# Norms of the later chunks for all heads at once: a fused attention and two-MLP kernel on one core

## The chip, the core and the metric

The kernel runs on one core of one Trainium2 chip. The engines named below are PE (TensorE matmul; PEld is its weight load, which overlaps PE), DVE (VectorE), ACT (ScalarE), POOL (GpSimd) and SP (SyncE), which here issues every transfer between the core's memory and the chip's main memory (DMA). The metric is device time in microseconds (us) of one execution, lower is better.

## What is computed

Cut to what matters, with batch 8, 8 heads, sequence 576, head width 64, so 4608 tokens of 512 values:

```python
kv  = einsum('bhsd,bhse->bhde', k, v)             # no softmax: one 64x64 matrix per head and batch
out = einsum('bhsd,bhde->bhse', q, kv)
rms = sqrt(mean(out * out, axis=-1) + 1e-06)      # over the 64 values of one head
x   = (out / rms * g_norm)                        # -> 4608 x 512
h   = x @ w_in;   x = max(0.01 * h, h) @ w_out            # first MLP, 512 -> 2048 -> 512
h   = x @ w_in2;  x = P(h) / (Q(h) + 1e-6) @ w_out2       # second MLP, P cubic, Q quadratic in |h|
```

## The kernel before

Values lie transposed: features on the 128 partitions, 512 tokens of a chunk in the free dimension. There are nine chunks (numbers 0 to 8) and four feature groups `p` of 128 (two heads each). The weights have 16 blocks of 128 hidden features. Every product of the two MLPs is three matmuls of 128x128 by 512 tokens on type float32r (`mm3`, lines 180 to 182: low weights by high x, high by high, high by low). One block's `emit_h` is 12 of them and its `emit_y` another 12.

A written list of steps, `STARTUP`, makes the attention part of chunks 0 and 1 and the first 6 blocks of both. Then come the units of the first MLP: unit 2 (rest of chunk 0), unit 3 (rest of chunk 1, 10 blocks), and one unit of 16 blocks for each of chunks 2 to 8. A block is a **slot**. In a slot the order on PE is: `emit_h` of the slot's block, `emit_y` of the block two slots earlier, and then what is planned at that slot with the word "pe". `prep(c, ...)` plans the attention part of the next chunk in the slots of the running unit: "load" is issued one slot ahead, "early" is recorded right after `emit_h`, "post" after "pe". The schedule is manual: each engine runs its instructions in the order in which they are written. The second MLP follows with its own loop over all nine chunks; the change doesn't touch it.

For the attention of one chunk `prep` needs, on PE in plain float32: the k v products of a batch (`mm_kv`, line 281, result `kvacc`; five token tiles, the last of 64 tokens, 8 logical matmuls for a pair of column halves each), and q times kv (`mm_out`, line 298, result `po`, once for each pair of feature groups, `mo`). In the before kernel the mean of squares is made for each feature group apart: ACT squares `po` and copies it, the square is split in a high and a low float32r part (ACT, DVE), and `mm_ms` (line 517) multiplies both parts by `ones`, a 128x128 block matrix of 1/64, so that the mean stands in all 64 rows of its head. Then `nm` makes the factor on [128, 512] for each group: two ACT steps (lines 303 and 304) and three DVE steps (lines 307, 308, 311), and splits x.

PSUM tiles of the attention part (`kvacc`, `po`, `pm`) share two banks under the tag "att". The core's four `raw` buffers are shared by the loads of q, k v, the second MLP's weights (32 transfers of 512 KB, three pairs a unit, narrowed on ACT and DVE into `cv` and stored back) and the stores of x.

In units 4 to 7 (chunks 2 to 5) the slots were: `mo` at 2 and 6, `ms` at 4 and 8 (two groups each), k v tiles at 10 (two), 12 (two) and 14 (the last). In unit 3: k v of one batch at 0 and 1, `mo` at 2 and 5, `ms` at 4 and 7, k v of the next batch at 8 and 9. Units 8 and 9 (chunks 6 and 7) have no k v left; the last unit prepares nothing.

Of the kernel before, what the change touches and what calls it, by code (L numbers as in the profile page):

```python
# [8 lines left out]
F32 = mybir.dt.float32  # L9
F32R = mybir.dt.float32r  # L10
U32 = mybir.dt.uint32
I64 = mybir.dt.int64
AF = mybir.ActivationFunctionType
ALU = mybir.AluOpType
# [3 lines left out]
P = 128  # L18
N = 512
# [3 lines left out]
c wu,30 kv,0,3,w0_8 kv,0,4,w0_9 w,2,1 kv,0,2,w0_10 kv,0,1,w0_11 q,0,0,w0_12 kv,0,0,w1_6 q,0,1,w1_7 km,0,3  # L23
    wu,3 km,0,4 wu,3 w,0,1 kv,1,3,w1_8 kv,1,2,w1_9 ab,2,1 g na,2,1 km,0,2 wu,3 w,0,0 kv,1,0,w0_6 kv,1,1,w0_7
    km,0,1 wu,3 hi,2,1 w,1,1 kv,1,4,w1_5 lo,2,1 q,1,0,raw q,1,1,raw w,2,0 km,0,0 wu,3 w,5,1 w,1,0 ev,0 po,0,0
    wu,3 po,0,1 wu,3 sq,0,1 sq,0,0 sq,0,3 pm,0,0 wu,6 sq,0,2 ab,0,1 pm,0,1 wu,6 na,0,1 km,1,3 nr,0 km,1,2 nw,0
    hi,0,1 w,3,1 ab,0,0 cg bc,0,0 na,0,0 oc,0,2,w0_9 oc,0,1,w0_8 km,1,0 oc,0,3,w0_9 oc,0,0,w0_8 km,1,1 xw,0,1
    w,3,0 hi,0,0 xw,0,0 xh,0,1 lo,0,0 ab,1,1 xh,0,0 xl,0,1 km,1,4 na,1,1 ev,1 bc,0,1 po,1,0 xw,0,3 hi,1,1 w,4,1
    xw,0,2 xh,0,3 lo,1,1 sq,1,0 xh,0,2 xl,0,3 po,1,1 sq,1,1 xl,0,2 oc,1,1,w0_10 pm,1,0 xl,0,0 ab,2,0 lo,0,1
    sq,1,3 h,0,0 na,2,0 oc,1,2,w0_11 oc,1,3,w0_11 sq,1,2 ab,1,0 w,5,0 hi,2,0 na,1,0 pm,1,1 oc,1,0,w0_10 lk,0,0  # L30
    h,0,1 lo,2,0 ab,3,1 w,4,0 nr,1 gl,0,0 na,3,1 ab,5,1 ab,3,0 y,0,0 lk,0,1 nw,1 w,6,1 hi,3,1 hi,1,0 na,5,1
    ab,5,0 bc,1,1 h,0,3 xw,1,3 hi,5,1 w,8,1 lo,1,0 xh,1,3 lo,3,1 ab,4,0 xl,1,3 ab,4,1 h,0,2 gl,0,1 xw,1,2
    lo,5,1 xh,1,2 na,3,0 y,0,1 lk,0,2 xl,1,2 w,6,0 hi,3,0 gl,0,2 lk,0,3 lo,3,0 bc,1,0 na,4,1 ab,6,1 y,0,2
    xw,1,0 hi,4,1 w,7,1 xw,1,1 ab,6,0 xh,1,0 lo,4,1 xh,1,1 h,0,4 xl,1,0 xl,1,1 gl,0,3 na,6,0 y,0,3 lk,0,4
# [7 lines left out]
def kernel(  # L42
# [36 lines left out]

    x2 = [dp.tile([P, NC, N], F32, tag=f"x2_{c}", name=f"x2_{c}") for c in range(NCH)]  # L80
    yp = [dp.tile([P, NC, N], F32, tag=f"yp_{c}", name=f"yp_{c}") for c in range(2)]
    w2f = [dp.tile([P, 2, NC * P], F32, tag=f"w2_{f}", name=f"w2_{f}") for f in range(NF)]


# [47 lines left out]
    def split(hi, lo, src, pool=False):  # L132

        nc.scalar.activation(out=hi, in_=src, func=AF.Copy)  # L134
        if pool:
            nc.gpsimd.tensor_tensor(out=lo, in0=src, in1=hi.bitcast(F32), op=ALU.subtract)  # L136
        else:
            split_lo(hi, lo, src)
# [59 lines left out]
    def new_x():  # L198
        return ([xp.tile([P, N], F32R, tag=f"xh{cc}", name=f"xh{cc}") for cc in range(NC)],
                [xp.tile([P, N], F32R, tag=f"xl{cc}", name=f"xl{cc}") for cc in range(NC)])  # L200
# [42 lines left out]
    with tc.manual_schedule():  # L243
        Y = {}
        G = {}
        with ExitStack() as actx:
# [37 lines left out]
            def evac_kv(bt, acc):  # L284
                KV[bt] = kvp.tile([P, NC, D], F32, tag="kv", name="kv")
                nc.scalar.copy(out=KV[bt], in_=acc[:, :NC * D].rearrange("p (c e) -> p c e", c=NC))
# [15 lines left out]
            def norm_act(m, r, w):  # L302
                nc.scalar.activation(out=r, in_=m, func=AF.Abs_reciprocal_sqrt, scale=MS_S, bias=lnb[:, 0:1])
                nc.scalar.activation(out=w, in_=r, func=AF.Square, scale=MS_R)

            def norm_dve(m, r, w):
                nc.vector.scalar_tensor_tensor(out=w, in0=m, scalar=EPS, in1=w, op0=ALU.add, op1=ALU.mult)
                nc.vector.scalar_tensor_tensor(out=w, in0=w, scalar=-3.0, in1=r, op0=ALU.add, op1=ALU.mult)

            def scaled(out, o, w):  # L310
                nc.vector.scalar_tensor_tensor(out=out, in0=o, scalar=gsc[:, 0:1], in1=w, op0=ALU.mult, op1=ALU.mult)


            order = []
            for f in range(NF + 3):
# [79 lines left out]
            def scratch(tag, n, name="s"):  # L395
                return tp.tile([P, N], F32, tag=tag, name=name, bufs=n)
# [2 lines left out]
                return (ps_h if at == "h" else ps_a if at == "att" else ps_y).tile([P, N], F32, tag=at, name=name)  # L399

            def leaky(ps):
                t = scratch("t", 4, "t")
                nc.scalar.activation(out=t, in_=ps, func=AF.Prelu, alpha=0.01)  # L403
                return t

# [22 lines left out]
            def p_po(c, g):  # L428
                for p in (2 * g, 2 * g + 1):
                    po[c, p] = bank(f"y{p}", "po")  # L430
                mm_out(c, g, qs.pop((c, g)), (po[c, 2 * g], po[c, 2 * g + 1]))

            def p_sq(c, p):
                ss[c, p] = scratch("sh" if p % 2 else "sl", 2)
                nc.scalar.activation(out=ss[c, p], in_=po[c, p], func=AF.Square)

            def p_oc(c, p, at):
# [3 lines left out]
                        xx[c, p // 2 * 2 + i] = t[:, i, :]  # L441
                nc.scalar.activation(out=xx[c, p], in_=po[c, p], func=AF.Copy, scale=gsc[:, 0:1])

            def p_pm(c, g):

                if c not in pm:
                    pm[c] = bank("att", "pm")
                for p in (2 * g, 2 * g + 1):
                    nc.tensor.matmul(out=pm[c][32 * p:32 * (p + 1)], lhsT=pick, rhs=ss.pop((c, p)), start=True, stop=True)  # L449

            def p_nr(c):
                rr[c], ww[c] = scratch("s", 1, "r"), scratch("o", 2, "w")
                norm_act(pm[c], rr[c], ww[c])

            def p_nw(c):
# [46 lines left out]
                name, *args = step.split(",")  # L502
                STEPS[name](*(int(x) if x.isdigit() else x for x in args))

            def sq_out(ps, o):

                s = tp.tile([P, N], F32, tag="s", name="s")
                nc.scalar.activation(out=s, in_=ps, func=AF.Square)
                nc.scalar.copy(out=o, in_=ps)
                hi = tp.tile([P, N], F32R, tag="sh", name="sh", bufs=2)  # L510
                lo = tp.tile([P, N], F32R, tag="sl", name="sl", bufs=2)
                split(hi, lo, s)
                return lo, hi

            def mm_ms(parts, dst):
                for i, x in enumerate(parts):
                    nc.tensor.matmul(out=dst, lhsT=ones, rhs=x, start=i == 0, stop=i == len(parts) - 1)  # L517

            def norm(o, ps):
                r = tp.tile([P, N], F32, tag="t", name="r", bufs=4)  # L520
                w = tp.tile([P, N], F32, tag="t", name="w", bufs=4)
                norm_act(ps, r, w)
                norm_dve(ps, r, w)
                scaled(w, o, w)
                return w

            def prep(c, out0, outs, bursts):

                slots = {}

                def at(s, when, fn, *args):
                    slots.setdefault(s, {}).setdefault(when, []).append(lambda: fn(*args))

                st = {}

                def ld(bt, i):
                    st["kv", i] = load_kv(bt, i)

                def mm(bt, i):
                    if i == 0:  # L540
                        acc[bt] = ps_a.tile([P, NC * P], F32, tag="att", name="kvacc")
                    mm_kv(i, st.pop(("kv", i)), acc[bt], i == 0, i == nk - 1)

                for s, bt, tiles in bursts:
                    for i in tiles:
                        at(s, "load", ld, bt, i)
                        at(s, "pe", mm, bt, i)
                        if i == nk - 1:
                            at(s, "post", lambda bt=bt: evac_kv(bt, acc.pop(bt)))

                def new():
                    X[c] = new_x()

                def ldq(g):
                    st["q", g] = load_q(c, g)

                def mo(g):
                    for p in (2 * g, 2 * g + 1):
                        st["po", p] = ps_a.tile([P, N], F32, tag="att", name="po")
                    mm_out(c, g, st.pop(("q", g)), (st["po", 2 * g], st["po", 2 * g + 1]))  # L560

                def so(p):
                    o = tp.tile([P, N], F32, tag="o", name="o", bufs=2)
                    st["s", p] = sq_out(st["po", p], o)
                    st["po", p] = o

                def ms(p):
                    st["pm", p] = ps_a.tile([P, N], F32, tag="att", name="pm")
                    mm_ms(st.pop(("s", p)), st["pm", p])

                def nm(p):
                    if p == 0:
                        new()
                    w = norm(st.pop(("po", p)), st.pop(("pm", p)))
                    split(X[c][0][p], X[c][1][p], w)

                lag = 2
                for g in range(NC // 2):
                    s = out0 + g * outs
                    at(s, "load", ldq, g)  # L580
                    at(s, "pe", mo, g)
                    for i in range(2):
                        p = 2 * g + i
                        at(s + 1, "early", so, p)
                        at(s + lag, "pe", ms, p)
                        at(s + lag + 1 + i * (outs - lag - 1), "early", nm, p)
                return slots

            def run_slot(slots, s, when):
# [22 lines left out]

            for ui, (c, f0, f1) in enumerate(units):
                slots = {}
                tiles = (0, 1), (2, 3), (4,)
                if ui < 2:
                    continue
                if ui == 3:
                    slots = prep(2, 2, 3, [*zip((0, 1, 1), (2, 2, 2), tiles), *zip((8, 9, 9), (3, 3, 3), tiles)])
                elif ui > 3 and c + 1 < NCH:  # L620
                    slots = prep(c + 1, 2, 4, [*zip((10, 12, 14), (c + 2,) * 3, tiles)] if c + 2 < B else [])
                last = ui == len(units) - 1
                for f in range(f0, f1):
                    sl = f - f0
# [187 lines left out]
```

## Time and profile before

| what | value |
|---|---|
| three runs | 1673.28, 1676.21, 1677.27 us, median 1676.21 |
| the profiled execution, its own time | 1677.88 us |
| its span, first to last instruction | 1675.8 us |
| PE busy | 1665.6 us, 99% of the span |
| DVE, ACT, POOL busy | 970.2, 853.6, 168.8 us |
| chain that ended last | PE 96%, DVE 2%, DMA 1% |
| granted TensorE clock | 1.0 in the stretches used below, that is 2.4 GHz |

Matmuls are pipelined, so a record of one is longer than the time that it takes from the stream. What a stretch of PE costs is read here from the starts of the matmuls on either side of it.

### The profile page before, as it was taken

The page shows a single profiled execution, that of the slowest core. Times are in us where ns is not written, and L with a number is a line of the kernel's source. Part 1 is how long each engine was busy: PE and PEld are TensorE (multiplying, and loading weights), DVE is VectorE, ACT ScalarE, POOL GpSimd, SP SyncE. Part 2 cuts the span into 40 slices and gives each one's busy share as a digit, 9 for nine tenths or more (in the row PEclk, how much of TensorE's full clock was granted, in tenths as well). Part 3 has the DMA queues.
Part 4 walks back from the last instruction along what each step waited for, and adds up shares of the span by engine and source line. Part 5 has one row for each costly group of instructions (what it writes and reads, how often), then busy time and mean ns, then how long its engine had stood idle before and what let it go on. Part 6 is the DMA issues. An engine that isn't in the chain of part 4 may idle for free.

```text
span 1675.8 us, 19355 instructions
## 1 busy us (share of the span) xinstructions
PE 1665.6 (99%) x7959; PEld 1355.1 (81%) x7959; DVE 970.2 (58%) x1132; ACT 853.6 (51%) x1150; POOL 168.8 (10%) x74
## 2 busy tenths in 40 slices
PE   8999999999999999999999999999999999999999
PEld 6688788878888887878888888888888888888887
DVE  3949335254352615342347767776767777777776
ACT  3636335253443425343347656666665666656565
POOL 0000000000000000000001122222122222212221
PEclk9999999999999999999999999999999999999999
DMA  9325434142322323020331010101010000101000
GB/s 250 127 88 178 144 91 128 57 139 82 112 86 86 114 72 110 26 89 0 122 106 63 1 51 1 50 1 51 1 48 4 26 26 1 50 1 50 1 25 25
DMA packets 38359, 112.39 MB, mean 67 GB/s; under 512 B 4480, under 2 KB 4480, under 8 KB 38272
## 3 DMA queue, kind: packets, MB, share of 16 engines
q1 hardware_dynamic: 38272, 111.17, 20.8%
q8 instruction: 62, 1.02, 0.3%
q14 instruction: 25, 0.20, 0.0%
HBM read 81.79 MB, written 29.36 MB: 66 GB/s over the span
## 4 chain that ended last, share of the span: by engine, by line
PE 96%; DVE 2%; DMA 1%; ACT 0%; SPq 0%; issue 0%
PE ph L180 16%; PE y L180 15%; PE y L182 15%; PE y L181 15%; PE ph L182 15%; PE ph L181 15%; PE kvacc L281 1%; PE po L298 1%; DMA raw<-in_kv_dram 1%; PE pm L517 1%; PE warm L411 0%; DVE w L130 0%; PE bc L462 0%; DVE tmp L165 0%; PE pm L449 0%; DVE tmp L168 0%
## 5 line engine op out<-in xcount | busy, mean ns | idle before, releaser
L180 PE MATMUL ph<-xh,w 128*128 128x512 f32 x1152 | 452.1, 392 | 1.0 <-DVE w L130 1.0
L182 PE MATMUL ph<-xl,w 128*128 128x512 f32 x1152 | 448.5, 389 | 0.0
L181 PE MATMUL ph<-xh,w 128*128 128x512 f32 x1152 | 448.5, 389 | 0.0
L180 PE MATMUL y<-gh,w 128*128 128x512 f32 x1152 | 448.4, 389 | 0.1
L181 PE MATMUL y<-gh,w 128*128 128x512 f32 x1152 | 448.2, 389 | 0.0
L182 PE MATMUL y<-gl,w 128*128 128x512 f32 x1152 | 448.1, 389 | 0.0
L136 POOL TENSOR_TENSOR gl<-p,gh 128x1024 fp32r<-128x1024 f32 x70 | 168.6, 2408 | 1482.6 <-ACT gh L134 1482.6
L130 DVE TENSOR_TENSOR gl<-t,gh 128x512 fp32r<-128x512 f32 x144 | 99.4, 691 | 351.5 <-ACT gh L639 330.9
L180 PEld LDWEIGHTS ph<-xh,w 128*128 128x128 f32 x1152 | 216.1, 188 | 54.9 <-issue 7.4
L180 PEld LDWEIGHTS y<-gh,w 128*128 128x128 f32 x1152 | 216.3, 188 | 46.0 <-ACT gh L483 0.8
L182 PEld LDWEIGHTS y<-gl,w 128*128 128x128 f32 x1152 | 216.3, 188 | 45.1 <-DVE gl L130 0.2
L182 PEld LDWEIGHTS ph<-xl,w 128*128 128x128 f32 x1152 | 216.2, 188 | 45.1
L181 PEld LDWEIGHTS ph<-xh,w 128*128 128x128 f32 x1152 | 216.5, 188 | 44.4
L181 PEld LDWEIGHTS y<-gh,w 128*128 128x128 f32 x1152 | 216.0, 188 | 44.8
L403 ACT ACTIVATE t<-ph 128x512 f32<-128x512 f32 x144 | 85.5, 594 | 314.5 <-PE ph L182 314.5
L690 ACT ACTIVATE e<-ph,bb 128x1024 f32<-128x1024 f32 (+1 forms) x73 | 80.6, 1105 | 291.2 <-PE ph L182 291.2
L693 DVE SCALAR_TENSOR_TENSOR e<-s,b,e 128x1024 f32<-128x1024 f32 (+1 forms) x73 | 92.6, 1269 | 176.6 <-ACT s L691 176.6
L701 DVE SCALAR_TENSOR_TENSOR e<-e,z 128x1024 f32<-128x1024 f32 (+1 forms) x73 | 104.8, 1436 | 30.6 <-ACT z L698 30.5
L700 DVE SCALAR_TENSOR_TENSOR p<-p,na,ph 128x1024 f32<-128x1024 f32 (+1 forms) x73 | 92.4, 1266 | 2.6
L702 DVE SCALAR_TENSOR_TENSOR p<-p,na,z 128x1024 f32<-128x1024 f32 (+1 forms) x73 | 91.9, 1259 | 0.0
L703 DVE SCALAR_TENSOR_TENSOR p<-e,p 128x1024 f32<-128x1024 f32 (+1 forms) x73 | 88.3, 1210 | 2.5
L699 DVE TENSOR_TENSOR p<-p,ph 128x1024 f32<-128x1024 f32 (+1 forms) x73 | 87.5, 1198 | 0.0
(83 smaller groups left out, 1248.7 us busy)
## 6 DMA issues: line engine op xcount, KB each, us to landing
raw<-in_kv_dram SPq DMA_DIRECT2D x32, 512.0 KB, 4.5
tmp<-in_w_dram SPq DMA_DIRECT2D x32, 512.0 KB, 5.6
raw<-in_w_dram SPq DMA_DIRECT2D x32, 512.0 KB, 6.1
raw<-in_qT_dram SPq DMA_DIRECT2D x36, 256.0 KB, 5.8
x<-raw SPq DMA_DIRECT2D x18, 512.0 KB, 3.4
raw<-x SPq DMA_DIRECT2D x18, 512.0 KB, 5.4
w<-cv SPq DMA_DIRECT2D x16, 512.0 KB, 2.9
raw<-w SPq DMA_DIRECT2D x32, 256.0 KB, 3.2
```

What stands on the lines that cost most here:

```text
L130: nc.vector.tensor_tensor(out=lo, in0=src, in1=hi.bitcast(F32), op=ALU.subtract)
L136: nc.gpsimd.tensor_tensor(out=lo, in0=src, in1=hi.bitcast(F32), op=ALU.subtract)
L180: nc.tensor.matmul(out=dst, lhsT=wl, rhs=xh, start=first, stop=False, **kw)
L181: nc.tensor.matmul(out=dst, lhsT=wh, rhs=xh, start=False, stop=False, **kw)
L182: nc.tensor.matmul(out=dst, lhsT=wh, rhs=xl, start=False, stop=last, **kw)
L403: nc.scalar.activation(out=t, in_=ps, func=AF.Prelu, alpha=0.01)
L693: nc.vector.scalar_tensor_tensor(out=e, in0=s, scalar=b1[:, 0:1], in1=e, op0=ALU.mult, op1=ALU.add)
L699: nc.vector.tensor_tensor(out=p, in0=p, in1=ph, op=ALU.mult)
L700: nc.vector.scalar_tensor_tensor(out=p, in0=p, scalar=na[:, 1:2], in1=ph, op0=ALU.add, op1=ALU.mult)
L701: nc.vector.scalar_tensor_tensor(out=e, in0=e, scalar=Q_C, in1=z, op0=ALU.add, op1=ALU.mult)
L702: nc.vector.scalar_tensor_tensor(out=p, in0=p, scalar=na[:, 0:1], in1=z, op0=ALU.add, op1=ALU.mult)
L703: nc.vector.scalar_tensor_tensor(out=p, in0=e, scalar=-2.0, in1=p, op0=ALU.add, op1=ALU.mult)
```

## The change

For chunks 2 to 8 the mean square is now made as chunks 0 and 1 already made it: ACT's squares of all four groups lie in one tile `sq`, and four plain float32 matmuls with `pick` (128x32; columns 0 and 1 hold 1/64 for one head each) put the means of all eight heads in one PSUM bank, group `p` in rows 32p and 32p+1. One `nm` makes the factor for all heads on one [128, 512] tile. A store writes it to main memory (`rs`), and two loads read it back so that each head's row stands in 64 partitions for all four groups. `sx` then multiplies and splits x for each group. The gain `g_norm` is applied by the ACT copy out of `po`. The slots move too: in units 4 to 7 `mo` at 2 and 5, `ms` with three k v tiles right behind it at 8, the spread at the end of slot 9, the other two k v tiles at 11, and the four `sx` at 12 to 15; in unit 3 `mo` at 2 and 3, `ms` with three tiles at 4, the spread at 5, two tiles at 7, `sx` at 8 and 9. Two scratch tiles of `STARTUP` get other homes, and the scratch `t` has 3 buffers in place of 4.

```diff
-            def mm_ms(parts, dst):
-                for i, x in enumerate(parts):
-                    nc.tensor.matmul(out=dst, lhsT=ones, rhs=x, start=i == 0, stop=i == len(parts) - 1)
+            def mm_ms(p, x, dst):
+                nc.tensor.matmul(out=dst[32 * p:32 * (p + 1)], lhsT=pick, rhs=x, start=True, stop=True)
...
-                t = scratch("t", 4, "t")
+                t = scratch("t", 3, "t")
...
+                def so(p):
+                    if p == 0:
+                        st["s"] = squares()
+                        st["o"] = tp.tile([P, NC, N], F32, tag="o", name="o")
+                    ps = st.pop(("po", p))
+                    nc.scalar.activation(out=st["s"][:, p, :], in_=ps, func=AF.Square)
+                    nc.scalar.activation(out=st["o"][:, p, :], in_=ps, func=AF.Copy, scale=gsc[:, 0:1])
+                def ms():
+                    st["m"] = ps_a.tile([P, N], F32, tag="att", name="pm")
+                    for p in range(NC):
+                        mm_ms(p, st["s"][:, p, :], st["m"])
+                def nm():
+                    r, w = scratch("t", 3, "r"), scratch("t", 3, "w")
+                    norm_act(st["m"], r, w)
+                    norm_dve(st.pop("m"), r, w)
+                    st["w"] = w
+                def spread_w():
+                    nc.sync.dma_start(out=rs[c], in_=st.pop("w"))
+                    t = st["b"] = squares()
+                    for j in range(P // D):
+                        nc.sync.dma_start(out=t[j * D:(j + 1) * D], in_=rs[c].rearrange("(p r) n -> r p n", r=32)[j:j + 1]
+                                          .to_broadcast([D, NC, N]))
+                def sx(p):
+                    if p == 0:
+                        X[c] = new_x()
+                    x = st["o"][:, p, :]
+                    nc.vector.tensor_tensor(out=x, in0=x, in1=st["b"][:, p, :], op=ALU.mult)
+                    split(X[c][0][p], X[c][1][p], x)
...
-                    slots = prep(2, 2, 3, [*zip((0, 1, 1), (2, 2, 2), tiles), *zip((8, 9, 9), (3, 3, 3), tiles)])
+                    slots = prep(2, (2, 3), 4, (8, 8, 9, 9), [(0, 2, (0, 1)), (1, 2, (2, 3, 4)), (4, 3, (0, 1, 2)), (7, 3, (3, 4))])
...
-                    slots = prep(c + 1, 2, 4, [*zip((10, 12, 14), (c + 2,) * 3, tiles)] if c + 2 < B else [])
+                    slots = prep(c + 1, (2, 5), 8, (12, 13, 14, 15), [(8, c + 2, (0, 1, 2)), (11, c + 2, (3, 4))] if c + 2 < B else [])
```

PE in the unit of chunk 2. Before, the means of two feature groups stand alone between the last `y` of a slot and the first `ph` of the next (slot 4), and the k v products of two tiles stand alone at slot 10.

```order
L182 MATMUL y_2088<-gl,w_2_579 128x512
L517 MATMUL pm<-sl,ones 128x512
L517 MATMUL pm<-sh,ones 128x512
L517 MATMUL pm<-sl,ones 128x512
L517 MATMUL pm<-sh,ones 128x512
L180 MATMUL ph<-xh_1728,w_5_762 128x512
```

In the changed kernel, slot 8 of the same unit:

```order
L183 MATMUL y_2046<-gl,w_6_1019 128x512
L448 MATMUL pm<-sq,pick 32x512 x4
L282 MATMUL kvacc<-raw 64x64 x24
L181 MATMUL ph<-xh_1884,w_9_1065 128x512
L182 MATMUL ph<-xh_1884,w_9_1065 128x512
```

The eight float32r matmuls of a chunk in two places became four plain float32 ones of 32 output rows in one place, with three k v tiles (24 logical matmuls) behind them.

SP, the only queue that issues transfers, in the same unit, from the second pair of weight loads on; `w_N<-cv` is the store of a narrowed weight block. Before:

```order
L209 DMA w_0_86<-cv 128x1024
L147 DMA raw<-in_w_dram 128x512 x4
L263 DMA raw<-in_kv_dram 128x1024 x2
L209 DMA w_1_87<-cv 128x1024
L263 DMA raw<-in_kv_dram 128x1024 x2
L263 DMA raw<-in_kv_dram 64x1024
L209 DMA w_2_88<-cv 128x1024
```

In the changed kernel:

```order
L148 DMA raw<-in_w_dram 128x512 x2
L264 DMA raw<-in_kv_dram 128x1024 x3
L148 DMA raw<-in_w_dram 128x512 x2
L210 DMA w_1_96<-cv 128x1024
L558 DMA rs_89<-w 128x512
L561 DMA sq<-rs_89 64x4x512 x2
L264 DMA raw<-in_kv_dram 128x1024
L264 DMA raw<-in_kv_dram 64x1024
L210 DMA w_2_97<-cv 128x1024
```

Three k v loads moved ahead of the third pair of weight loads, and the store and the two spreading loads now stand ahead of the last two k v loads.

## Rows read from the trace of the kernel before

**Rows 1.** Page, parts 1 and 4: PE's busy time; the last chain by engine.

```profile
PE 1665.6 (99%) x7959; PEld 1355.1 (81%) x7959; DVE 970.2 (58%) x1132; ACT 853.6 (51%) x1150; POOL 168.8 (10%) x74
...
PE 96%; DVE 2%; DMA 1%; ACT 0%; SPq 0%; issue 0%
```

**Rows 2.** Windows: busy us (instructions) of PE, PEld, DVE, ACT, POOL; clock, DMA, GB/s.

```profile
445.00:540.00 95.00, 95.00 (x506) 76.94 (x505) 39.33 (x62) 37.95 (x67) 0.00 (x0) 1.00 0.31 98
900.00:1500.00 600.00, 600.00 (x2649) 496.82 (x2648) 438.86 (x365) 371.23 (x392) 134.24 (x56) 1.00 0.07 25
```

**Rows 3.** Chain in order of time, one unit: start, us, what.

```profile
440.03 1.02 PE po L298 x16
...
452.15 0.92 PE pm L517 x4
...
487.91 1.08 PE kvacc L281 x32
```

**Rows 4.** Timeline of PE, around old means (four matmuls lie between): start, us, instruction.

```profile
356.91 0.39 PE L182 MATMUL y<-gl,w 128*128 128x512 f32 x1
...
358.29 0.40 PE L181 MATMUL ph<-xh,w 128*128 128x512 f32 x1
```

**Rows 5.** PE and PEld at `STARTUP`'s last means, two `pick` matmuls; then by tile.

```profile
50.77 0.39 PE L182 MATMUL ph<-xl,w 128*128 128x512 f32 x1
51.09 1.05 PE L449 MATMUL pm<-s,pick 128*32 128x512 f32 x4
...
52.40 0.39 PE L181 MATMUL ph<-xh,w 128*128 128x512 f32 x1
...
51.08 0.14 PEld L449 LDWEIGHTS pm<-s,pick 128*32 128x32 f32 x4 [0.35 <-ACT w L365]
...
L449 PE MATMUL pm<-s,pick x4: 592/604/617, 51.1 to 51.5; 128*32 128x512 f32 x4
```

**Rows 6.** Timeline of PE around two full k v tiles (kvacc x32 between).

```profile
392.67 0.39 PE L182 MATMUL y<-gl,w 128*128 128x512 f32 x1
...
394.40 0.39 PE L181 MATMUL ph<-xh,w 128*128 128x512 f32 x1
```

**Rows 7.** Timeline of PE around the last k v tile alone (kvacc x16 between).

```profile
417.04 0.39 PE L182 MATMUL y<-gl,w 128*128 128x512 f32 x1
...
418.31 0.39 PE L181 MATMUL ph<-xh,w 128*128 128x512 f32 x1
```

**Rows 8.** Timeline of PE around two full tiles and the last (kvacc x48 between).

```profile
231.67 0.39 PE L182 MATMUL y<-gl,w 128*128 128x512 f32 x1
...
234.02 0.40 PE L181 MATMUL ph<-xh,w 128*128 128x512 f32 x1
```

**Rows 9.** Timeline of PE and PEld around unit 3's second `mo` (po x16 between).

```profile
205.97 0.39 PE L182 MATMUL y<-gl,w 128*128 128x512 f32 x1
...
208.10 0.40 PE L181 MATMUL ph<-xh,w 128*128 128x512 f32 x1
...
206.75 0.42 PEld L298 LDWEIGHTS po<-raw,kv 64*64 64x64 f32 x14 [0.28 <-DVE w L307]
```

**Rows 10.** Timeline of PE around a `mo` of unit 4 (po x16 between).

```profile
344.79 0.39 PE L182 MATMUL y<-gl,w 128*128 128x512 f32 x1
...
346.46 0.40 PE L181 MATMUL ph<-xh,w 128*128 128x512 f32 x1
```

**Rows 11.** DMA issues (KB each, us to landing); GB/s in 40 slices, 393 to 413 us.

```profile
raw<-in_kv_dram SPq DMA_DIRECT2D x32, 512.0 KB, 4.5
...
out_dram<-raw SPq DMA_DIRECT2D x4, 256.0 KB, 2.1
...
GB/s 0 0 0 131 131 311 418 402 418 402 385 57 0 0 0 0 0 0 0 0 0 0 0 0 0 0 16 0 0 319 393 336 115 369 262 225 78 0 0 0
```

**Rows 12.** Tile `pm`: ACT's and DVE's steps on it, ns minimum, median, maximum.

```profile
L303 ACT ACTIVATE r<-pm,lnb x30: 669/682/689, 32.3 to 763.1; 128x512 f32<-128x512 f32 x30
L307 DVE SCALAR_TENSOR_TENSOR w<-pm,w x30: 681/691/693, 33.7 to 764.5; 128x512 f32<-128x512 f32 x30
```

More of the change, by code (lines that the diff above doesn't have):

```diff
@@ L25 @@
     km,0,1 wu,3 hi,2,1 w,1,1 kv,1,4,w1_5 lo,2,1 q,1,0,raw q,1,1,raw w,2,0 km,0,0 wu,3 w,5,1 w,1,0 ev,0 po,0,0
-    wu,3 po,0,1 wu,3 sq,0,1 sq,0,0 sq,0,3 pm,0,0 wu,6 sq,0,2 ab,0,1 pm,0,1 wu,6 na,0,1 km,1,3 nr,0 km,1,2 nw,0
+    wu,3 po,0,1 wu,3 sq,0,1 sq,0,0 sq,0,3 pm,0,0 wu,6 sq,0,2 ab,0,1 pm,0,1 wu,6 na,0,1 km,1,3 nr,0,w0_12 km,1,2 nw,0
     hi,0,1 w,3,1 ab,0,0 cg bc,0,0 na,0,0 oc,0,2,w0_9 oc,0,1,w0_8 km,1,0 oc,0,3,w0_9 oc,0,0,w0_8 km,1,1 xw,0,1
@@ L30 @@
     sq,1,3 h,0,0 na,2,0 oc,1,2,w0_11 oc,1,3,w0_11 sq,1,2 ab,1,0 w,5,0 hi,2,0 na,1,0 pm,1,1 oc,1,0,w0_10 lk,0,0
-    h,0,1 lo,2,0 ab,3,1 w,4,0 nr,1 gl,0,0 na,3,1 ab,5,1 ab,3,0 y,0,0 lk,0,1 nw,1 w,6,1 hi,3,1 hi,1,0 na,5,1
+    h,0,1 lo,2,0 ab,3,1 w,4,0 nr,1,w1_7 gl,0,0 na,3,1 ab,5,1 ab,3,0 y,0,0 lk,0,1 nw,1 w,6,1 hi,3,1 hi,1,0 na,5,1
     ab,5,0 bc,1,1 h,0,3 xw,1,3 hi,5,1 w,8,1 lo,1,0 xh,1,3 lo,3,1 ab,4,0 xl,1,3 ab,4,1 h,0,2 gl,0,1 xw,1,2
@@ L81 @@
     yp = [dp.tile([P, NC, N], F32, tag=f"yp_{c}", name=f"yp_{c}") for c in range(2)]
+    rs = [dp.tile([P, N], F32, tag=f"rs_{c}", name=f"rs_{c}") for c in range(NCH)]
     w2f = [dp.tile([P, 2, NC * P], F32, tag=f"w2_{f}", name=f"w2_{f}") for f in range(NF)]
@@ L308, in norm_dve @@
                 nc.vector.scalar_tensor_tensor(out=w, in0=w, scalar=-3.0, in1=r, op0=ALU.add, op1=ALU.mult)
-            def scaled(out, o, w):
-                nc.vector.scalar_tensor_tensor(out=out, in0=o, scalar=gsc[:, 0:1], in1=w, op0=ALU.mult, op1=ALU.mult)
             order = []
@@ L431, in p_po, with squares @@
                 mm_out(c, g, qs.pop((c, g)), (po[c, 2 * g], po[c, 2 * g + 1]))
+            def squares():
+                return tp.tile([P, NC, N], F32, tag="sq", name="sq")
             def p_sq(c, p):
-                ss[c, p] = scratch("sh" if p % 2 else "sl", 2)
+                if ("sq", c) not in ss:
+                    ss["sq", c] = squares()
+                ss[c, p] = ss["sq", c][:, p, :]
                 nc.scalar.activation(out=ss[c, p], in_=po[c, p], func=AF.Square)
@@ L448, in p_pm, with p_nr @@
                 for p in (2 * g, 2 * g + 1):
-                    nc.tensor.matmul(out=pm[c][32 * p:32 * (p + 1)], lhsT=pick, rhs=ss.pop((c, p)), start=True, stop=True)
-            def p_nr(c):
-                rr[c], ww[c] = scratch("s", 1, "r"), scratch("o", 2, "w")
+                    mm_ms(p, ss.pop((c, p)), pm[c])
+            def p_nr(c, at):
+                t = home(at)
+                rr[c], ww[c] = t[:, 0, :], t[:, 1, :]
                 norm_act(pm[c], rr[c], ww[c])
@@ L503, with prep @@
                 STEPS[name](*(int(x) if x.isdigit() else x for x in args))
[L505 to L513, printed above, removed]
-            def mm_ms(parts, dst):
-                for i, x in enumerate(parts):
-                    nc.tensor.matmul(out=dst, lhsT=ones, rhs=x, start=i == 0, stop=i == len(parts) - 1)
[L519 to L527, printed above, removed]
+            def prep(c, po_at, ms_at, x_at, bursts):
                 slots = {}
@@ L542, in mm @@
                     mm_kv(i, st.pop(("kv", i)), acc[bt], i == 0, i == nk - 1)
[L544 to L552, printed above, removed]
                 def ldq(g):
@@ L562, in so @@
                 def so(p):
[L563 to L571, printed above, removed]
-                    if p == 0:
-                        new()
-                    w = norm(st.pop(("po", p)), st.pop(("pm", p)))
-                    split(X[c][0][p], X[c][1][p], w)
@@ L577, in prep @@
-                lag = 2
-                for g in range(NC // 2):
[L579 to L586, printed above, removed]
+                    if p == 0:
+                        st["s"] = squares()
+                        st["o"] = tp.tile([P, NC, N], F32, tag="o", name="o")
@@ new lines, in prep @@
+                for g in range(NC // 2):
+                    at(po_at[g], "load", ldq, g)
+                    at(po_at[g], "pe", mo, g)
+                    for p in (2 * g, 2 * g + 1):
+                        at(po_at[g] + 1, "early", so, p)
+                at(ms_at, "pe", ms)
+                at(ms_at + 1, "early", nm)
+                at(ms_at + 1, "post", spread_w)
+                for p in range(NC):
+                    at(x_at[p], "early", sx, p)
+                for s, bt, tiles in bursts:
+                    for i in tiles:
+                        at(s, "load", ld, bt, i)
+                        at(s, "pe", mm, bt, i)
+                        if i == nk - 1:
+                            at(s, "post", lambda bt=bt: evac_kv(bt, acc.pop(bt)))
@@ L614 @@
                 slots = {}
-                tiles = (0, 1), (2, 3), (4,)
                 if ui < 2:
```

## The prediction

> **What bounds the kernel now.** The page comes first: PE is busy for 99% of the span and carries 96% of the chain that ended last [rows 1]. The windows say the same of the stretch that the change touches: in the 95 us from 445 us on PE is busy throughout, DVE for 39.33 us and ACT for 37.95 us [rows 2]. So what the change takes from ACT and DVE is worth nothing by itself, and what it takes from PE's stream comes off the end, one for one, as long as no new wait appears there. A busy share can't price that, since records of pipelined matmuls overlap; starts can. In the long stretch without attention work 2649 matmuls fit into 600 us; two of them only reach in from the edges, which gives 600 / 2647 = 0.2267 us for one MLP matmul [rows 2]. A slot of 24 is 5.44 us. The chain in order of time then shows the pattern of a unit: now and then a run of `po`, `pm` or `kvacc` stands between two slots [rows 3].
>
> I price every such run in one way: from the start of the last MLP matmul before it to the start of the second one behind it, less 2 x 0.2267 = 0.453 us. The second, because the first MLP matmul after a float32 run is longer too.
>
> **The prices.**
> - Old means of two groups, four float32r matmuls: 358.29 - 356.91 = 1.38, so 0.927 us [rows 4]. That is four times the ordinary pace; entering and leaving costs nothing.
> - `pick` means of two groups, plain float32: 52.40 - 50.77 = 1.63, so 1.177 us [rows 5].
> - Two full k v tiles: 1.73, so 1.277 us [rows 6]; the last tile alone: 1.27, so 0.817 us [rows 7]. The 16 extra records of the second tile cost 0.46, so entering and leaving a float32 run costs 0.817 - 0.46 = 0.357 us.
> - Two full tiles and the last: 2.35, so 1.897 us [rows 8]. The last tile, of half height, costs 0.62 behind a full one, 0.16 more than a tile.
> - `mo`: 1.67, so 1.217 us [rows 10]. The second `mo` of unit 3: 2.13, so 1.677 us, and PEld waits there for line 307, the norm of the group before, which still reads a PSUM bank [rows 9].
>
> **The change part by part.**
>
> (1) *The old means go.* Seven chunks with two runs each: 14 x 0.927 = 12.98 us less.
>
> (2) *The new means come.* The trace has no run of four `pick` matmuls, only of two. There each logical matmul is two records; the four records begin between 51.1 and 51.5, last some 0.6 each, and the run is over after 1.05 us [rows 5], so the two matmuls go side by side. In 1.02 us `po` brings through as many columns on four quarters of the array as four logical matmuls of 512 [rows 3]. I take it that four column strips overlap as two do and as the four quarters of `po` do. A run of four then costs what a run of two costs, 1.177 us. Chunks 7 and 8 (made in units 8 and 9 of the list, chunks 6 and 7) have no k v products left, so there it stands alone: 2 x 1.177 = 2.35 us more.
>
> (3) *The joint.* For the other five chunks k v tiles follow at once, so entering and leaving is counted with the k v run. The low end for the means is 1.177 - 0.357 = 0.82. The high end is 1.177: the joint saves nothing. Between the strips of 32 columns and the halves of 64 the shape of the array's use changes, and the one such change inside a run that the trace shows, from full to half-height k v tiles, cost 0.16 [rows 6 to 8]. So I take 0.82 + 0.16 = 0.98, and 5 x 0.98 = 4.90 us more. The Trainium skill bears on this (TensorEngine Tiling, Key Properties): a change of tiling mode, not just of tile, drains the engine. By that rule each joint pays one more drain, and if a drain is half of entering and leaving, an estimate of 0.82 + 0.18 = 1.00 results, a tenth of a us more over five joints; the 0.16 of the half-height tile agrees with it.
>
> (4) *k v products in two runs in place of three*, units 4 to 7. Before: 1.277 + 1.277 + 0.817 = 3.37. After: three full tiles 1.277 + 0.46 = 1.74, and a full one with the last 1.277 + 0.16 = 1.44, together 3.17. That saves 0.20 x 4 = 0.79 us. The two batches of unit 3 had two runs each and keep them, cut 3 and 2 where one was cut 2 and 3: nothing.
>
> (5) *The wait of unit 3.* `po` no longer needs a bank that a norm still reads: its banks come free when ACT has made four steps of some 0.6 us in slot 3, and PE reaches `mo` only 24 matmuls, 5.44 us, after the first. I take the 0.46 as gone; the other end is that it stays.
>
> (6) *ACT and DVE* lose ten and eight steps a chunk, of about 0.69 us each [rows 12]. Worth nothing: both idle for over half of the stretch [rows 2]. In the startup steps only homes of scratch tiles change, with nothing added on an engine: nothing.
>
> (7) *The spread*: a store of 256 KB, two loads of 512 KB, and SP is held until the store has landed. Priced at nothing, since slots cover it. Counted from the start of slot 9: ACT and DVE need four steps of 0.69 [rows 12], so the store goes out by about 3 us, if a step or two stands ahead. A 256 KB store landed 2.1 us after its issue [rows 11]. The second pair of weight loads and a weight store, 1.5 MB, are ahead of it in the queue; at 400 GB/s [rows 11] they take 3.9 us from the end of slot 8. So the spreading loads go out at 5 to 7 us and land 4.5 us [rows 11] or a little more later, at 10 to 13. `sx` begins with slot 12, at 16.3 us. Without that cover DVE would stand in front of the MLP's own steps, yet `emit_y` trails by two slots, 10.9 us more.
>
> Behind the spread on SP stand the last two k v loads, which PE needs at the end of slot 11, again at 16.3 us. Going out at 6 to 8 us they land at 11 to 15: hidden, by the smallest margin of the change. In unit 3 the distances are the same (spread at 5, k v at 7, `sx` from 8), and there no weights of the second MLP stand in the queue.
>
> Sum: - 12.98 + 2.35 + 4.90 - 0.79 - 0.46 = **- 6.98 us**. From the profiled execution, 1677.88 us, that is 1670.9. This execution lies 1.67 above the median of the three runs, so against the median I expect **1669.2 us**, 0.42% less. With the joint at its ends (0.82, 1.18) and the wait kept, the gain runs from 5.5 to 7.8.
>
> **The rivals.**
>
> *A. Strips overlap only in pairs.* For: the trace shows two, never four, of 128 rows by 32 columns. Against: four quarters do overlap in `po` [rows 3]. Price: a second pass of 0.82 in each of seven runs, 5.7 us; the gain shrinks to 1.2, the time is 1675.0.
>
> *B. Matmuls on the same rows don't overlap at all.* Three further passes of 0.82 in each of seven runs are 17.2 us, so 10.2 us slower than before, 1686.4. Against it: in the pair all four weight loads are over within 0.14 us, while the first matmul, begun at 51.09, still runs, and both groups are through 1.05 us after that start [rows 5]. The Trainium skill has a rule from which this follows (TensorE: Matmul & The Clock Gate, Part 3): weight loads overlap running matmuls only where their row groups differ. The `pick` matmuls all use all rows, so by it they would go one after another. The pair's row contradicts it, so it gets little chance.
>
> *C. The last k v tiles come late (the other side).* Place: end of slot 11 in units 4 to 7, where PE would wait for `raw<-in_kv`. Between slot 8's end and their landing 3.7 MB must pass (weights 1.57 with the store, the spread 1.31, k v 0.79). At 418 GB/s that is 9 us, but the same row has slices of 225 [rows 11], and at such a rate it is 16.3 us plus the wait for the store's landing, 2 us: 2 us late. The gain is used up at 1.75 us a unit, and beyond 3.0 us the kernel is slower by over 0.3%. At 4 us late it would be 9 us slower, some 1685.
>
> *D. The means don't matter because PE isn't the limit there.* Against it stands the full window [rows 2]; I give it no chance of its own.
>
> **How the numbers follow.** The forecast gets 0.80, A 0.09, B 0.03, C 0.08 (half of it no change, half slower). The forecast's own range is 1667 to 1672: its bounds, and the scatter of the runs, 4 us between the three shown. Between faster and no change a measurement can tell about 0.3%, 5 us: the forecast's 7 is over that bound with some 0.93. So faster 0.74; same 0.06 + 0.09 + 0.04 = 0.19; slower 0.03 + 0.04 = 0.07. The range that holds 8 in 10 reaches to A: 1666 to 1676.
>
> **What the profile after would show.** A run of `pm` alone with chunks 7 and 8: about 1.0 us long from its start to the next `ph`; 1.8 would be A, 3.5 B. A joined run of `pm` and `kvacc`: 0.98 + 1.74 = 2.7 us added; k v of two tiles 1.44. No idle time on PE or PEld before `kvacc` for `raw<-in_kv`; any is C. The second `mo` of unit 3 at 1.22. ACT and DVE lose 70 and 56 steps, and the end moves by PE's terms alone. The prediction is wrong if the four strips don't overlap, or if a k v load lands after its slot.

## The result, and the profile after

The changed kernel took 1685.66 us (median of six runs, 1682.38 to 1692.09) beside 1675.49 us for the kernel before on the same chips: ratio 1.0068, 95% interval 1.0044 to 1.0093. It is slower, by 10 us, where 7 us less were forecast, and it lies above the range of 1666 to 1676. The profiled execution took 1686.85 us.

The page of the changed kernel, parts 1 and 4, beside [rows 1]:

```profile
PE 1659.1 (98%) x7959; PEld 1346.7 (80%) x7959; DVE 917.7 (54%) x1062; ACT 817.6 (49%) x1080; POOL 168.8 (10%) x74
...
PE 90%; DMA 7%; DVE 2%; ACT 1%; SPq 1%; issue 0%
PE ph L181 15%; PE ph L182 15%; PE ph L183 15%; PE y L181 15%; PE y L182 15%; PE y L183 14%; DMA raw<-in_kv_dram 5%; DMA rs<-w 2%; PE po L299 1%; PE kvacc L282 1%; PE pm L448 0%; DVE tmp L166 0%; SPq L561 0%; DVE w L131 0%; DVE tmp L169 0%
```

PE is busy 6.5 us less although the span is 9.3 us longer, and two transfers have entered the last chain: the k v loads with 5% and the factor store with 2%. A share of the chain isn't idle time of PE: the chain goes through a transfer from its issue to its landing, while PE still has other work. In unit 4 it reads, in order of time (start, us, what):

```profile
285.26 6.12 DMA rs<-w
...
291.40 0.59 SPq L561
...
293.40 11.64 DMA raw<-in_kv_dram
```

Where they stand is seen in the timeline of PE in unit 4: the joined run at slot 8, the k v run at slot 11, and the means that stand alone for chunk 8 (start, us, instruction, idle time before it and what ended it).

```profile
280.98 0.39 PE L183 MATMUL y<-gl,w 128*128 128x512 f32 x1
281.30 1.07 PE L448 MATMUL pm<-sq,pick 128*32 128x512 f32 x8
282.29 1.62 PE L282 MATMUL kvacc<-raw 128*64 128x64 f32 x48
283.84 0.50 PE L181 MATMUL ph<-xh,w 128*128 128x512 f32 x1
284.18 0.40 PE L182 MATMUL ph<-xh,w 128*128 128x512 f32 x1
...
300.07 0.39 PE L183 MATMUL y<-gl,w 128*128 128x512 f32 x1
303.09 0.69 PE L282 MATMUL kvacc<-raw 128*64 128x64 f32 x16 [2.63 <-DMA raw<-in_kv_dram]
305.08 1.12 PE L282 MATMUL kvacc<-raw 64*64 64x64 f32 x16 [1.31 <-DMA raw<-in_kv_dram]
306.13 0.79 PE L181 MATMUL ph<-xh,w 128*128 128x512 f32 x1
306.72 0.63 PE L182 MATMUL ph<-xh,w 128*128 128x512 f32 x1
307.14 0.63 PE L183 MATMUL ph<-xl,w 128*128 128x512 f32 x1
...
765.71 0.39 PE L183 MATMUL y<-gl,w 128*128 128x512 f32 x1
766.03 1.06 PE L448 MATMUL pm<-sq,pick 128*32 128x512 f32 x8
767.03 0.50 PE L181 MATMUL ph<-xh,w 128*128 128x512 f32 x1
767.36 0.39 PE L182 MATMUL ph<-xh,w 128*128 128x512 f32 x1
```

The new work costs what was forecast: the means alone add 767.36 - 765.71 - 0.453 = 1.20 us (1.177 taken), the joined run 284.18 - 280.98 - 0.453 = 2.75 (0.98 + 1.74 = 2.72 taken). The second k v run is the trouble: PE stands for 2.63 us before the first of its tiles and for 1.31 us before the second, each time until a k v load lands; 306.72 - 300.07 - 0.453 = 6.20 us in place of 1.44. Units 5, 6 and 7 do the same, with 1.7 to 3.1 us between the last `y` and the first k v matmul.

Behind the wait the MLP matmuls start 0.42 to 0.43 us apart, not 0.227. The windows of the same stretch say why (busy us and instructions of PE, PEld, DVE, ACT, POOL, then granted clock, DMA share, GB/s; the page's row of clock tenths doesn't show it):

```profile
281.00:300.40 19.40, 19.40 (x130) 15.07 (x128) 7.43 (x13) 5.57 (x9) 0.00 (x0) 1.00 0.61 171
300.40:303.00 2.60, 0.05 (x1) 0.00 (x0) 0.69 (x1) 0.00 (x0) 0.00 (x0) 1.00 0.50 137
303.00:306.10 3.10, 1.71 (x32) 1.48 (x32) 0.00 (x0) 0.00 (x0) 0.00 (x0) 0.64 0.03 7
306.10:311.00 4.90, 4.90 (x14) 3.87 (x13) 0.69 (x1) 0.90 (x2) 0.00 (x0) 0.53 0.00 0
311.00:340.00 29.00, 29.00 (x130) 23.98 (x129) 9.70 (x16) 10.03 (x17) 0.00 (x0) 1.00 0.13 37
```

The granted clock is 1.00 up to 303.00 us, 0.64 in the mean over the second wait and its tiles, and 0.53 in the 4.9 us of full work behind that: it has gone from the 2.4 GHz level nearly to the 1.2 GHz one. So the waits of this unit cost more than their own length; how much more is told below.

What SP did before the wait, in the changed kernel's timeline:

```profile
282.99 0.80 SPq L148 DMA_DIRECT2D raw<-in_w_dram  x2
283.84 0.42 SPq L210 DMA_DIRECT2D w<-cv  x1
285.26 0.33 SPq L558 DMA_DIRECT2D rs<-w  x1
291.40 1.25 SPq L561 DMA_DIRECT2D sq<-rs  x2
292.75 1.96 SPq L264 DMA_DIRECT2D raw<-in_kv_dram  x2
```

Its issues from 281 to 307 us (KB each, us from issue to landing):

```profile
sq<-rs SPq DMA_DIRECT2D x2, 512.0 KB, 8.0
raw<-in_kv_dram SPq DMA_DIRECT2D x1, 512.0 KB, 10.3
rs<-w SPq DMA_DIRECT2D x1, 256.0 KB, 6.1
raw<-in_kv_dram SPq DMA_DIRECT2D x1, 256.0 KB, 11.6
```

The store lands 6.1 us after its issue; until then SP issues nothing. Then the spreading loads go out, and 1.35 us behind them the k v loads, which need 10.3 and 11.6 us where 4.5 was the median before [rows 11]. They land at 303.0 and 305.0; PE was ready at 300.4.

### The profile page after: what moved, and what is told of

Its sections match the earlier page's. It is cut to its first block, busy times and chain, and to the rows that moved or that the text cites. A ratio compares the mean times of both kernels' runs of the same rounds, so it can differ in the third digit from the quotient of the medians.

```text
span 1685.1 us, 19277 instructions
## 1 busy us (share of the span) xinstructions
PE 1659.1 (98%) x7959; PEld 1346.7 (80%) x7959; DVE 917.7 (54%) x1062; ACT 817.6 (49%) x1080; POOL 168.8 (10%) x74
## 4 chain that ended last, share of the span: by engine, by line
PE 90%; DMA 7%; DVE 2%; ACT 1%; SPq 1%; issue 0%
PE ph L181 15%; PE ph L182 15%; PE ph L183 15%; PE y L181 15%; PE y L182 15%; PE y L183 14%; DMA raw<-in_kv_dram 5%; DMA rs<-w 2%; PE po L299 1%; PE kvacc L282 1%; PE pm L448 0%; DVE tmp L166 0%; SPq L561 0%; DVE w L131 0%; DVE tmp L169 0%
```

## The experiments

Theories: (1) the k v loads are late only because they stand on SP behind the store's landing and the spread; (2) the spread is slow because it fetches the same rows 64 times; (3) the new form is dear on PE by itself. Theories (2) and (3) would ask for another spread or for the old means; (1) for another order.

The single runs of the kernel before lie between 1671.2 and 1677.7 us, and in the traces most of such a scatter lies in the startup (last section). So beside the ratio, taken to runs of the kernel before on the same chip, the table gives what the trace shows free of it: the span less the start of unit 3's first k v run (for the kernel before 1675.8 - 173.21 = 1502.6), and what the second k v run of unit 4 adds (1.44 forecast). There is one trace for each kernel.

| run | median us | ratio to before, 95% interval | from that run to the end, us | second k v run adds, us |
|---|---|---|---|---|
| before | 1675.49 | 1 | 1502.6 | three runs |
| changed | 1685.66 | 1.0068 (1.0044 to 1.0093) | 1515.3 | 6.2 |
| k v loads first | 1667.70 | 0.9961 (0.9945 to 0.9976) | 1496.2 | 1.43 |
| second k v run at 14 | 1668.49 | 0.9962 (0.9948 to 0.9976) | 1496.9 | 1.43 |
| no wait for the store | 1668.75 | 0.9960 (0.9946 to 0.9974) | 1496.5 | 1.43 |
| the same, distinct rows | 1667.83 | 0.9960 (0.9946 to 0.9973) | 1495.7 | 1.44 |
| spread issued by POOL | 1668.88 | 0.9959 (0.9945 to 0.9974) | 1496.3 | 1.43 |
| means alone | 1667.36 | 0.9953 (0.9938 to 0.9968) | 1498.7 | three runs |
| quarter of the spread | 1666.76 | 0.9952 (0.9938 to 0.9965) | 1496.7 | 1.42 |
| loads first in unit 3 too | 1665.92 | 0.9946 (0.9933 to 0.9958) | 1496.5 | 1.43 |
| two k v runs alone | 1697.38 | 1.0138 (1.0122 to 1.0154) | 1527.1 | 1.43 (the first 5.7) |
| unit 3 cut three and two | 1668.01 | 0.9961 (0.9949 to 0.9974) | 1495.4 | 1.43 |

**The k v loads ahead of the spread.**

```diff
-                        at(s, "load", ld, bt, i)
+                        at(s - (s == 11), "load", ld, bt, i)
```

> The changed kernel with one thing moved: in units 4 to 7 the loads of the last two k v tiles are issued one slot earlier, so they stand on SP ahead of the factor store and the two spreading loads, not behind them. Theory 1 (place in the queue: PE waits at slot 11 only because these loads stand behind the store's landing and the spread): no wait at the joint of slot 11, the two-tile run adds 1.44 us, and the sum of the prediction comes through, about 7 us under the kernel before (ratio 0.996), near 1669. The spreading loads land 1 to 3 us later than in the changed kernel and nobody waits for them. Rival (theory 3: the new form itself is dear on PE, through the joint or the clock, whatever the loads do): still 5 us or more over the kernel before, 1680 or more.

Theory (1) holds and (3) falls: the same instructions on PE, ACT and DVE and the same bytes, two loads issued a slot earlier, and the kernel goes from 10 us over the one before to some 6 us under it. PE at slot 11 of its unit 4 has no wait left:

```profile
296.27 0.39 PE L183 MATMUL y<-gl,w 128*128 128x512 f32 x1
296.58 1.30 PE L282 MATMUL kvacc<-raw 128*64 128x64 f32 x32
297.81 0.50 PE L181 MATMUL ph<-xh,w 128*128 128x512 f32 x1
298.15 0.40 PE L182 MATMUL ph<-xh,w 128*128 128x512 f32 x1
```

**The second k v run later.** Its edit: `(14, c + 2, (3, 4))` in place of `(11, c + 2, (3, 4))`.

> The changed kernel with the second k v run of units 4 to 7 at slot 14 in place of 11; its loads go out with slot 13. Theory 1: the spread is over by then, no wait for the k v loads, about 7 us under the kernel before, like the run with the loads moved ahead. Theory 3: 1680 or more. If DVE's wait for the spread mattered too, this run would keep it (the spreading loads land as in the changed kernel, some 18 us after slot 9 begins) and stay above the other.

The same result by more distance in place of another order. SP doesn't follow the slots of PE here: in unit 4 it issues the two k v loads right behind the spread, as in the changed kernel, and not with slot 13; only PE's need for them comes three slots later. DVE still waits for the spread (four waits, 5.5 us together; 11.5 us in the run before this one, where the spread lands later), and that costs nothing that the time can tell: the traces of these two runs end within 0.7 us of each other, counted from unit 3's first k v run.

**The spread without its wait, and with distinct rows.** The lines of the edits are joined here; the second added one, behind the dots, is that of the distinct rows.

```diff
-in_=rs[c].rearrange("(p r) n -> r p n", r=32)[j:j + 1].to_broadcast([D, NC, N])
+in_=qT[0:P, c * N:(c + 1) * N].rearrange("(p r) n -> r p n", r=32)[j:j + 1].to_broadcast([D, NC, N])
...
+in_=qT[j * NC * D:(j + 1) * NC * D, c * N:(c + 1) * N].rearrange("(p r) n -> r p n", r=D)
```

> The changed kernel, but the spreading loads read four rows of q, each 64 times, in place of the stored factors (so x is scaled by other numbers, and the output is not the reference's). Shape and bytes are the same; they no longer wait for the store to land. Theory 1: SP is held no longer, the k v loads go out about 6 us earlier and the wait at slot 11 goes or falls under 1 us: near 1669 to 1671. Theory 2 (the spread is slow because each row is fetched 64 times): the spreading loads still take 8 us or more from issue to landing, about as long as in the changed kernel, and the k v loads behind them 8 us or more; a wait of 0 to 1 us is left.

> As the run without the store's wait, but the spreading loads read 256 different rows of q each, in pieces of the same 2 KB (output not the reference's). Theory 2: they land at least 2 us sooner after issue than those that fetch each row 64 times. Theory 1: the same within 1 us, since what takes time is the bytes ahead in the queue. Time near 1669 by both.

The issues of both in unit 4, first with repeated, then with distinct rows (KB each, us to landing):

```profile
sq<-in_qT_dram SPq DMA_DIRECT2D x2, 512.0 KB, 8.9
raw<-in_kv_dram SPq DMA_DIRECT2D x1, 512.0 KB, 10.2
```

```profile
sq<-in_qT_dram SPq DMA_DIRECT2D x2, 512.0 KB, 9.0
raw<-in_kv_dram SPq DMA_DIRECT2D x1, 512.0 KB, 10.3
```

8.9 and 9.0 us: fetching a row 64 times is no dearer than fetching 64 different ones, and theory (2) falls. The k v loads still need 10 us, but with the repeated rows they go out 4.1 us after slot 9 begins in place of 8.9, and PE doesn't wait.

**The spread issued by POOL.** The edit: `nc.gpsimd.dma_start` for the store and the two loads.

> The changed kernel with the factor store and the two spreading loads issued by POOL, which is idle in this stage, and not by SP. Bytes, order of work and the wait of the spread for its store are kept; only SP is no longer held while the store lands. If holding SP is what makes the k v loads late: they go out some 6 us sooner and the wait at slot 11 goes (two-tile run 1.44 us added), about 6 to 7 us under the kernel before. If the transfers of the spread by themselves crowd the k v loads out, a wait of 1 us or more is left in units 4 to 7.

The wait goes. Bytes and dependence are as in the changed kernel and SP is free, but a second thing differs: the spread now goes through a DMA queue of its own, so the k v loads no longer stand behind it in one queue. In unit 4 they go out 0.5 us after slot 9 begins and land 8.9 and 9.4 us after issue, in time. What of the gain belongs to which of the two this run doesn't tell.

**A quarter of the spread.** The edit: rows of group 0 alone (`[j:j + 1, 0:1]`, `to_broadcast([D, 1, N])`), used for all groups.

> The changed kernel with the two spreading loads cut to a quarter: only the first feature group's rows are spread, and all four groups are scaled with them (output not the reference's). SP is held for the store as before; 0.26 MB in place of 1.05 MB stand ahead of the k v loads. If the held SP alone were enough to make them late, the wait at slot 11 of 2 to 3 us stays. If it takes the spread's bytes as well, the k v loads land 4 to 6 us sooner than in the changed kernel and the wait is gone: 6 to 7 us under the kernel before.

Its issues in unit 4:

```profile
raw<-in_kv_dram SPq DMA_DIRECT2D x1, 512.0 KB, 5.2
rs<-w SPq DMA_DIRECT2D x1, 256.0 KB, 6.2
sq<-rs SPq DMA_DIRECT2D x2, 128.0 KB, 3.0
raw<-in_kv_dram SPq DMA_DIRECT2D x1, 256.0 KB, 5.6
```

SP is held for 6.2 us as before, yet the k v loads land 5.1 and 6.0 us sooner after issue (5.2 and 5.6 for 10.3 and 11.6). So it takes both: the held queue alone is harmless here, and so are the spread's bytes alone (the run without the store's wait).

**The means alone**, k v runs at 10, 12 and 14 as before.

> The new means and the spread, but the k v products in the slots of the kernel before (10, 12 and 14; 8 and 9 in unit 3), so no joined run. By the prices of the prediction: seven runs of means at 1.20 us in place of fourteen at 0.93, and the k v runs as before, that is 5 us under the kernel before; beside the joined version this costs 2 us, 0.8 for the third k v run and 1.2 for five joints. If the k v loads of slots 10 and 12 are held by the spread too, a wait shows there and the gain is gone.

No wait shows before its k v runs in unit 4 (1.29, 1.28 and 0.81 us added). Counted from unit 3's first k v run it gains 3.9 us, where 5 were expected; most of what is missing is the first `mo` of unit 3, which adds 2.10 us here and 1.25 in the kernel before. Against the version with joined runs and the loads first everywhere (1496.5), whose first `mo` adds 2.09, it is 2.2 us longer, where 2 were expected. The ratios can't tell the two apart.

**The two k v runs alone**, on the kernel before: `[(10, c + 2, (0, 1, 2)), (13, c + 2, (3, 4))]`.

> The kernel before with one part of the change: in units 4 to 7 the k v products in two runs, three tiles at slot 10 and two at slot 13, old means, no spread. By the prices of the prediction the runs add 1.74 and 1.44 us in place of 1.28, 1.28 and 0.82: 0.8 us less over four units, which time cannot tell from no change (ratio 1.000 within 0.002). If longer runs or their loads cost something of their own, a wait before the run or a higher price shows.

The price of the two runs was expected and a wait named as the other outcome; I did not see it coming, and it is the largest loss of all, 24 us: over the four units 17.5 in the k v runs and 6.5 in slow matmuls behind them. The timeline of PE in its unit 4, below it that of SP, and then what SP waited for from 273 to 297 us (us in total, times, longest):

```profile
294.96 1.15 PE L281 MATMUL kvacc<-raw 128*64 128x64 f32 x32
299.74 0.69 PE L281 MATMUL kvacc<-raw 128*64 128x64 f32 x16 [3.62 <-DMA raw<-in_kv_dram]
300.36 0.65 PE L180 MATMUL ph<-xh,w 128*128 128x512 f32 x1
```

```profile
273.52 22.50 SPq L263 DMA_DIRECT2D raw<-in_kv_dram  x3
...
SPq L263 <- DVE cv L168: 11.9, 2, 10.9
SPq L263 <- PE kvacc L281: 10.4, 1, 10.4
```

SP is at the three loads of slot 10 for 22.5 us: there the four `raw` buffers also hold a pair of weight loads. SP first waits for their narrowing on DVE, and the last of the three goes out only when PE has worked through a tile of the run that needs it. So three tiles at once don't fit between the weight loads of slot 8 and their narrowing. In the change the three loads stand ahead of that pair, and its three-tile runs don't wait in units 4 to 7.

**The loads first in unit 3 too, and its first batch cut three and two.** The edits: `at(s - (s in (7, 11)), ...)`, and with it `(0, 2, (0, 1, 2)), (1, 2, (3, 4))`.

> The version with the k v loads ahead of the spread in units 4 to 7, and now in unit 3 too, where the two-tile run still added 1.6 to 1.8 us in place of 1.44. Expected 0.2 to 0.4 us under that version, which time cannot tell but the run's price in the trace can (1.44), and about 7 us under the kernel before.

> The version with the k v loads ahead of the spread everywhere, and in unit 3 the first batch cut three and two in place of two and three, so that the buffers of the reloaded partial sums come free a slot sooner and the q loads of the first product with kv stand less deep in the queue. That product should add 1.2 to 1.3 us in place of 2.1; the rest as in the version without it: 7 to 8 us under the kernel before (ratio 0.995). If a wait comes before the third k v tile of slot 0 instead, the gain is gone again.

Both beat both kernels: ratios 0.9946 and 0.9961 to the one before, intervals that overlap. The two-tile run of unit 3 now adds 1.43 us, as expected. In the trace the second is 1.1 us shorter: its first `mo` of unit 3 adds 1.23 us in place of 2.09, where PE had waited for a q load. That the new cut took this wait away isn't shown, since the same `mo` adds 1.28 and 1.23 us with the old cut in the traces of "k v loads first" and "distinct rows", and 2.47 in two others. For one kernel to keep, either will do.

## Why the prediction was wrong

1. *What bounds the kernel*: right. PE's stream sets the end; whatever delayed it came off, or on, one for one.
2. *Terms (1) to (4)*: right. Means alone 1.20 for 1.177; three k v tiles alone 1.75 for 1.74 (unit 3 of the last version) and two 1.42 to 1.44 for 1.44, where nothing is late; so the joint 1.00 (2.75 - 1.75) for 0.98. Strips of 32 columns overlap four at a time: eight records in 1.06 us, as four had taken 1.05 [rows 5]. Rivals A and B fall with that; the rule of the Trainium skill behind B (TensorE: Matmul & The Clock Gate, Part 3), as B read it, doesn't hold for strips of columns here. Its drain at a change of tiling mode (TensorEngine Tiling, Key Properties) agrees, 1.00 by the estimate and 1.00 measured, but the 0.98 of the other working lies too near to be told from it.
3. *Term (5)*: half right. The second `mo` lost its wait (1.23), but the first, 1.25 in the kernel before, added 1.78 us in the changed kernel and took the 0.46 back. Over the traces of the versions with the same work up to there it adds 1.23 to 2.47 us, and in five of them PE waits there for a q load; why it scatters is open. *Term (6)* miscounted DVE: it lost 70 steps (1132 to 1062), not 56, worth nothing as forecast.
4. *Term (7)*, "Priced at nothing, since slots cover it": **this step failed**. Counted from the start of slot 9 (283.84 in unit 4) the two k v loads were to land at 11 to 15 us, with 16.3 as the need; they landed at 19.2 and 21.2, and PE was ready at 16.5. The store's landing was near the estimate (spreading loads out from 7.6, 5 to 7 forecast). The size that was off is the transfers behind it: from issue to landing about 4.5 us or a little more for the spread and 5 to 7 for the k v loads, and 6 to 10 and 10 to 12 measured. I had taken the median landing of other loads and 400 GB/s, the top of a row that also shows 225 [rows 11]. From the first spreading load's issue to the last landing 1.84 MB took 13.6 us, 135 GB/s; at 400 that is 4.6 us.
5. *Rival C* named the place, the engine and the transfer. It had 0.08 because I let the better rate decide. Its own working at 225 GB/s was still too short: 18.3 us from the end of slot 8 to the last landing, 21.2 measured (283.84 to 305.04). That its case of 4 us late gave 1685 is in part luck: the late loads added 13.8 us over the four units and not 16, and another 5.0 came from something that C had not priced, the clock's fall behind the longer waits. The unit of chunk 2, from its joined run to the next `mo`, took 65.25 us (281.30 to 346.55) where the version with the loads first takes 58.64; the wait and its run account for 4.8 of these 6.6 (6.20 for 1.44), the slow matmuls after it for 1.8.

The account closes: over the four units the changed kernel loses 6.6, 5.6, 1.7 and 4.9 us, 18.8 together, and 0.7 in unit 3; with the forecast's -7.0 that makes +12.5, and +12.7 is measured from unit 3's first k v run (1515.3 - 1502.6). Where neither a k v load nor the first `mo` is late the forecast sum is met: 1495.4 - 1502.6 = -7.2 us in the last version.

Not settled: why the spreading loads pass at a lower rate than others. Even in the version with all loads first, with nothing behind them in the queue, they land 5.7 and 7.4 us after issue. The repeat of rows is excluded. The size of their pieces (2 KB, where k v loads move 4 KB) and their 64 partitions (128 for most k v loads) were not tried apart.

## What to carry to other kernels

When a change puts a dependent store and load on an in-order queue, list what is queued behind it, and price those transfers with the bytes ahead of them at the poor rate of the trace, not the best one: here a margin that I had put at 1 to 5 us was gone, and even the poor rate was too good. Issue the loads that a busy engine needs soon ahead of the ones that have time; one line of order was worth 18 us. And a run is not joined for free because its matmuls are cheaper together: its buffers must be free at that place.

## What the runs showed of the hardware that was not expected

- The granted clock fell with the waits of PE in units 4, 5 and 7 and not in unit 6. In the changed kernel PE waited for 2.63 and 1.31 us in unit 4, for 2.71 in unit 5, for 1.28 and 0.33 in unit 6, and for 2.61 and 0.49 in unit 7. Unit 4 is shown above (0.53 in 4.9 us of full work). Units 5 to 7 in the same columns, behind their waits:

```profile
406.00:411.00 5.00, 5.00 (x15) 3.97 (x16) 0.69 (x1) 1.17 (x3) 0.00 (x0) 0.63 0.00 0
504.00:510.00 6.00, 6.00 (x28) 4.98 (x27) 3.12 (x6) 1.93 (x4) 0.00 (x0) 1.00 0.00 0
601.00:606.00 5.00, 5.00 (x17) 3.96 (x16) 0.69 (x1) 1.34 (x4) 0.00 (x0) 0.68 0.00 0
```

- Most of the scatter lies in the startup: the first k v run of unit 3 begins between 166.3 and 173.4 us, while in the seven versions that differ only in the spread or in when their k v loads or the second k v run come, and have no load late in units 4 to 7, the rest agrees within 1.2 us. Most of that 1.2 us lies in one place, the first `mo` of unit 3 (1.23 to 2.47 us added). So a difference of 1 us can be read from a trace where medians of whole runs can't show it, if the place that makes it is looked up. The changed kernel's own six runs spread over 9.7 us, more than those of any other version; only one of them has a trace, so how late the loads were in the others isn't known.
